# Column order of the output products, and the start of the large tiles, in an attention and expert kernel

## The chip, the core and the metric

The kernel runs on one core of one Trainium2 chip. The metric is the device time of one execution in microseconds (us); lower is better.

## The reference

Four batches of 3008 tokens with 256 features go through squared-ReLU attention and then through one gated expert layer:

```python
scores = (1 / S) * z @ z.T            # per batch, z is S x 64, S = 3008
attn = maximum(scores, 0) ** 2
x = u * (attn @ v)                    # S x 256
xn = x / rms(x) * g
g_ = xn @ w_gate                      # 256 x 1536
val = xn @ w_val                      # 256 x 1536
out = (silu(g_) * val) @ w_out        # 1536 x 256
```

All inputs and the output are float32.

## The kernel before, in words

The tokens of a batch are taken in pairs of chunks, 1024 tokens at a time (960 in the last pair of a batch): 12 pairs. A pair has two phases. Phase A is attention: for each of 24 blocks of 128 keys the scores are formed (L456, L457), squared, split into a rounded high part and the rest, and multiplied with the values (L585, L586, L590), which are split in the same way. Phase M is the expert layer, 12 units per pair: a unit takes 128 of the 1536 hidden features. With a seven-product scheme for 2 x 2 blocks it forms gate and value of both halves of the pair (L792 to L794; three matmuls to a product, for the high and low parts of weights and of tokens), applies SiLU, multiplies, and splits the result into a high part hH (ScalarE, L804) and a low part hL (VectorE, L809). All these matmuls take float32r operands and are written out in full precision into PSUM.

The change touches the output products, `Unit.y(h)`, called for h = 0 and h = 1. It multiplies the 128 hidden features of the unit with w_out and adds into two accumulators (d = 0, 1, 128 output features each) that stay open over the 12 units of a pair. Each call issues six matmuls: L820 (high weights woh, hH) and L821 (low weights wol, hH) for d = 0, the same for d = 1, then L824 (woh, hL) for both d. n is the number of moving columns, 512, or 480 in the last pair of a batch. The calls wait in a queue, `pend`, and are popped between the products of the next unit (L880, L886), so the order of matmuls on TensorE (PE) is written out by hand. After the last unit the accumulators are copied out (L833, L835) and stored (L836).

PE runs its instructions in the order written. Loads of weights and data come by DMA from SyncE's queue. The remaining engines form the scores' squares, splits and gates beside PE.

Memory: the tile pools lie one behind another in the order in which they are opened: const, keep, work, moving. Const holds front (96 floats), woh and wol (12,288 bytes each), misc and fold_sb (512 bytes each), in this order, per partition. Almost every tile of the other pools is 2048 or 4096 bytes long; the first tile of keep begins at byte 42,496, that is 41 x 1024 + 512, so these tiles all begin 512 bytes past a multiple of 1024. woh begins at 16,896, 512 past such a multiple too. fold_sb is read by one small matmul for each pair (L670). moving holds the tiles hH and hL (tags H and L) that the output products stream.

Of the kernel before, what the change touches and what calls it, by code (L numbers as in the profile page):

```python
# [8 lines left out]
F32 = mybir.dt.float32  # L9
# [10 lines left out]
P = 128  # L20
# [10 lines left out]
def kernel(  # L31
# [13 lines left out]
    nc = tc.nc  # L45
# [5 lines left out]
    NF = DFF // P  # L51
# [17 lines left out]
    const = ctx.enter_context(tc.tile_pool(name="const", bufs=1))  # L69
    keep = ctx.enter_context(tc.tile_pool(name="keep", bufs=1))  # L70
    work = ctx.enter_context(tc.tile_pool(name="work", bufs=1))

    moving = ctx.enter_context(tc.tile_pool(name="moving", bufs=1))
    ps_s = ctx.enter_context(tc.tile_pool(name="ps_s", bufs=4, space=bass.MemoryType.PSUM))
    ps_a = ctx.enter_context(tc.tile_pool(name="ps_a", bufs=1, space=bass.MemoryType.PSUM))
    dram = ctx.enter_context(tc.tile_pool(name="dram", bufs=1, space=bass.MemoryType.DRAM))
# [4 lines left out]
    def where(p):  # L81

        b, j = divmod(p, NP)
        return b, 2 * j, b * S + j * PAIR, min(PAIR, S - j * PAIR)
# [5 lines left out]
    woh = const.tile([P, NF, D], F32R, name="woh")  # L90
    wol = const.tile([P, NF, D], F32R, name="wol")
    misc = const.tile([P, P], F32, name="misc")
    g_sb, warm = front[:, :ND], front[:, ND:ND + 1]
    fold_sb = const.tile([P, P], F32, name="fold_sb")

    jobs = defaultdict(list)

# [110 lines left out]
    def prep_proj(j, pool, tags):  # L208
# [35 lines left out]
        def combine(key, x, y, op, into=None):  # L244
            def go():
                out = w[into] if into is not None else work.tile([P, CH], F32, tag="ws", name="ws")
                pool_pieces(out, w[x], w[y], op)
                w[key] = out
            return go
# [319 lines left out]
    acc = {}  # L569
# [64 lines left out]
    def norm_jobs(p):  # L634
# [3 lines left out]
        q = {}  # L638
        small = misc.rearrange("p (k a) -> p k a", a=PAIR // BLK)
        m, y, w, pp = (small[:, k, :nb] for k in range(4))  # L640
        x = [ux[p, d] for d in range(ND)]

# [36 lines left out]
        def cubic():  # L679
            nc.vector.tensor_tensor(w, m, y, op=ALU.mult)  # L680
            yield
            nc.vector.tensor_tensor(w, w, y, op=ALU.mult)
            yield
            nc.vector.tensor_scalar(pp, w, 0.375, -1.25, op0=ALU.mult, op1=ALU.add)
            yield
            nc.vector.tensor_tensor(pp, pp, w, op=ALU.mult)
            yield
            nc.vector.scalar_tensor_tensor(y, pp, 1.875, y, op0=ALU.add, op1=ALU.mult)
# [94 lines left out]
    class Unit:  # L783
# [28 lines left out]
        def y(self, h):  # L812
            p, f, n = self.p, self.f, self.n
            if f == 0:
                for d in range(ND):
                    acc[h, d] = ps_a.tile([P, CH], F32, tag=f"acc{h}{d}", name="py")
            hi, lo = self.h[h]
            for d in range(ND):
                ds = slice(d * P, (d + 1) * P)
                nc.tensor.matmul(acc[h, d][:, :n], woh[:, f, ds], hi[:, :n], start=(f == 0), stop=False)  # L820
                nc.tensor.matmul(acc[h, d][:, :n], wol[:, f, ds], hi[:, :n], start=False, stop=False)  # L821
            for d in range(ND):
                ds = slice(d * P, (d + 1) * P)
                nc.tensor.matmul(acc[h, d][:, :n], woh[:, f, ds], lo[:, :n], start=False, stop=(f == NF - 1))  # L824
            if f == NF - 1:
                t0 = where(p)[2] + h * n
                for d in range(ND):
                    if p == NPAIR - 1 and h == d == 1:
                        out = work.tile([P, CH], F32, tag="T", name="y", bufs=6)
                    else:  # L830
                        out = work.tile([P, CH], F32, tag="out", name="y", bufs=3)
                    if d == 0:
                        nc.scalar.copy(out[:, :n], acc[h, d][:, :n])  # L833
                    else:
                        nc.vector.tensor_copy(out[:, :n], acc[h, d][:, :n])  # L835
                    nc.sync.dma_start(out=outT[d * P:(d + 1) * P, t0:t0 + n], in_=out[:, :n])  # L836
# [172 lines left out]
    for p in range(NPAIR):  # L1009
        b, c0 = where(p)[:2]  # L1010
# [79 lines left out]
    for p in range(1, NPAIR):  # L1090
# [12 lines left out]
        start = 1  # L1103
# [5 lines left out]
        elif p == 2:  # L1109
            start = 4  # L1110
        elif p == NPAIR - 1:
            at(m.phase, 0, lambda p=p: load_x(p))
            start = 3
        h = m.put(jobs_, start)
# [133 lines left out]
```

## Time and profile before

| | |
|---|---|
| two timed executions | 2022.31 and 2023.12 us, median 2022.71 |
| span of the profiled execution (first to last instruction) | 2020.6 us |
| its own time apart from the span | not listed |
| mean granted TensorE clock | 0.999 |
| PE busy | 2006.9 us, 99% |
| VectorE (DVE) busy | 1604.6 us, 79% |
| ScalarE (ACT) busy | 1413.7 us, 70% |
| GpSimd (POOL) busy | 227.5 us, 11% |

PE's matmuls are pipelined: a matmul's duration in the profile reaches past the start of the next one. A rate is therefore read from the starts of successive matmuls. PEld is PE's loading of weights, which runs beside the matmuls. In the rows, "128x512 f32" behind a matmul is its output, 128 partitions by 512 columns. L820 is line 820 of the kernel before.

### The profile page before, as it was taken

How to read it: one execution, taken by the hardware profiler on the slowest of the kernel's cores; microseconds unless marked ns; L12 is line 12 of the kernel's file. 1: busy time of each engine (PE TensorE's matmuls, PEld its weight loads, DVE VectorE, ACT ScalarE, POOL GpSimd, SP SyncE). 2: the span in 40 equal slices, each digit the busy share in tenths (PEclk: the TensorE clock that was granted, in tenths of full speed). 3: DMA queues.
4: the chain of work that ended last, by engine and by line, in shares of the span. 5: the costliest groups of instructions: out<-in, count | busy, mean ns of one | idle time of the engine just before them, and what ended most of it. 6: DMA issues, size and time to landing. Idle time of an engine off the chain costs nothing.

```text
span 2020.6 us, 27263 instructions
## 1 busy us (share of the span) xinstructions
PE 2006.9 (99%) x8976; PEld 1675.6 (83%) x8976; DVE 1604.6 (79%) x2693; ACT 1413.7 (70%) x2580; POOL 227.5 (11%) x376
## 2 busy tenths in 40 slices
PE   9999999999999999999999999999999999999999
PEld 7787878888888888888888888888888888888887
DVE  8989978987867768787786877888778777777765
ACT  8888867886765656796586665779658656566665
POOL 0547905000000001300000000320000000000000
PEclk9999999999999999999999999999999999999999
DMA  5135575373494697246348478625536747734342
GB/s 173 48 112 169 133 241 172 136 233 128 113 237 151 158 204 238 102 170 215 125 132 233 139 160 228 213 102 189 180 120 184 205 135 181 196 128 165 115 147 93
DMA packets 352367, 328.38 MB, mean 163 GB/s; under 512 B 221536, under 2 KB 268256, under 8 KB 352224
## 3 DMA queue, kind: packets, MB, share of 16 engines
q1 hardware_dynamic: 352224, 326.64, 53.6%
q8 instruction: 70, 1.15, 0.2%
q14 instruction: 73, 0.60, 0.1%
HBM read 189.73 MB, written 85.72 MB: 136 GB/s over the span
## 4 chain that ended last, share of the span: by engine, by line
PE 92%; DMA 2%; DVE 2%; issue 1%; POOL 1%; ACT 1%; SPq 0%; DVEq 0%; POOLq 0%; ACTq 0%
PE po L585 11%; PE po L586 11%; PE ps L793 11%; PE ps L792 11%; PE po L590 11%; PE ps L794 11%; PE py L820 6%; PE py L821 6%; PE py L824 6%; PE ps L457 4%; PE ps L456 4%; DMA wu<-wc 1%; POOL w L140 1%; POOL wolo L140 1%; DVE L L508 0%
## 5 line engine op out<-in xcount | busy, mean ns | idle before, releaser
L585 PE MATMUL po<-H,vh 128*128 128x512 f32 (+1 forms) x1152 | 446.7, 388 | 1.9 <-DVE y L835 1.0
L586 PE MATMUL po<-H,vl 128*128 128x512 f32 (+1 forms) x1152 | 445.0, 386 | 0.0
L799 ACT COPY s<-ps 128x512 f32<-128x512 f32 (+1 forms) x432 | 249.6, 578 | 215.2 <-PE ps L794 214.6
L793 PE MATMUL ps<-xh,wu 128*128 128x512 f32 (+1 forms) x1008 | 389.3, 386 | 1.7 <-DMA wu<-wc 1.6
L792 PE MATMUL ps<-xh,wu 128*128 128x512 f32 (+1 forms) x1008 | 390.0, 387 | 0.5 <-DMA wu<-wc 0.5
L794 PE MATMUL ps<-xl,wu 128*128 128x512 f32 (+1 forms) x1008 | 388.6, 386 | 0.0
L590 PE MATMUL po<-L,vh 128*128 128x512 f32 (+1 forms) x1104 | 336.5, 386 | 3.1 <-DVE L L508 2.9
L804 ACT CAST hH<-s 128x512 fp32r<-128x512 f32 (+1 forms) x288 | 176.6, 613 | 194.5 <-DVE s L891 187.5
L809 DVE TENSOR_TENSOR hL<-s,hH 128x512 fp32r<-128x512 f32 (+1 forms) x288 | 200.0, 694 | 100.0 <-ACT hH L804 88.6
L468 ACT ACTIVATE r<-ps 128x512 f32<-128x512 f32 x354 | 195.9, 595 | 105.3 <-PE ps L457 87.6
L585 PEld LDWEIGHTS po<-H,vh 128*128 128x128 f32 x1152 | 216.3, 188 | 45.9 <-ACT H L495 2.1
L586 PEld LDWEIGHTS po<-H,vl 128*128 128x128 f32 x1152 | 216.5, 188 | 39.8
L475 DVE TENSOR_TENSOR r<-ps,r 128x512 f32<-128x512 f32 (+1 forms) x287 | 186.5, 681 | 73.1 <-ACT r L468 72.3
L590 PEld LDWEIGHTS po<-L,vh 128*128 128x128 f32 x1104 | 206.5, 188 | 45.4 <-DVE L L508 6.5
L508 DVE TENSOR_TENSOR L<-r,H 128x512 fp32r<-128x512 f32 (+1 forms) x334 | 226.7, 712 | 9.7 <-ACT r L502 7.5
L820 PE MATMUL py<-hH,woh 128*128 128x512 f32 (+1 forms) x576 | 222.2, 386 | 0.1
L821 PE MATMUL py<-hH,wol 128*128 128x512 f32 (+1 forms) x576 | 222.0, 385 | 0.0
L793 PEld LDWEIGHTS ps<-xh,wu 128*128 128x128 f32 x1008 | 189.2, 188 | 38.8 <-DMA wu<-wc 3.7
L792 PEld LDWEIGHTS ps<-xh,wu 128*128 128x128 f32 x1008 | 189.2, 188 | 38.8 <-ACT s L799 1.9
L794 PEld LDWEIGHTS ps<-xl,wu 128*128 128x128 f32 x1008 | 189.2, 188 | 35.9
L370 POOL TENSOR_TENSOR vl<-raw,vh 128x128 fp32r<-128x128 f32 x144 | 78.8, 586 | 938.5 <-ACT vh L359 484.4
L824 PE MATMUL py<-hL,woh 128*128 128x512 f32 (+1 forms) x576 | 175.3, 385 | 0.0
(96 smaller groups left out, 2973.7 us busy)
## 6 DMA issues: line engine op xcount, KB each, us to landing
wu<-wc SPq DMA_DIRECT2D x288, 448.0 KB, 4.0
kept<-halves SPq DMA_DIRECT2D x168, 256.0 KB, 2.2
raw<-in_v SPq DMA_DIRECT2D x44, 256.0 KB, 3.5
raw<-in_zT SPq DMA_DIRECT2D x38, 256.0 KB, 4.5
u<-in_uT SPq DMA_DIRECT2D x36, 256.0 KB, 4.6
xg<-u SPq DMA_DIRECT2D x36, 256.0 KB, 2.2
out_T<-y SPq DMA_DIRECT2D x32, 256.0 KB, 2.0
ux<-xg SPq DMA_DIRECT2D x14, 512.0 KB, 4.4
```

Of the source, the lines that this page charges most:

```text
L508: nc.vector.tensor_tensor(lo[:, :n], a[:, :n], f32(hi[:, :n]), op=ALU.subtract)
L585: nc.tensor.matmul(po[d][:, :n], wh[:, j, ds], hi[:, :n], start=(i == 0), stop=False)
L586: nc.tensor.matmul(po[d][:, :n], wl[:, j, ds], hi[:, :n], start=False, stop=(ends and lo is None))
L590: nc.tensor.matmul(po[d][:, :n], wh[:, j, ds], lo[:, :n], start=False, stop=ends)
L792: nc.tensor.matmul(ps[:, :n], wh[:, o, :], xh[:, :n], start=start, stop=False, skip_group_check=True)
L793: nc.tensor.matmul(ps[:, :n], wl[:, o, :], xh[:, :n], start=False, stop=False, skip_group_check=True)
L794: nc.tensor.matmul(ps[:, :n], wh[:, o, :], xl[:, :n], start=False, stop=stop, skip_group_check=True)
L799: nc.scalar.copy(s, ps[:, :self.n])
L809: nc.vector.tensor_tensor(lo[:, :self.n], s, f32(self.h[h][0][:, :self.n]), op=ALU.subtract)
L820: nc.tensor.matmul(acc[h, d][:, :n], woh[:, f, ds], hi[:, :n], start=(f == 0), stop=False)
L821: nc.tensor.matmul(acc[h, d][:, :n], wol[:, f, ds], hi[:, :n], start=False, stop=False)
L824: nc.tensor.matmul(acc[h, d][:, :n], woh[:, f, ds], lo[:, :n], start=False, stop=(f == NF - 1))
```

## The change

The three kinds of output product pass over the n columns in other orders than from left to right. The moving operand and the accumulator are permuted alike, so each column's sum still lands in its place. L820 takes the four quarters in the order 0, 2, 1, 3. L821 takes four columns of the first half, then four of the second half, and so on. L824 does the same with n / 16 columns at a time (32, or 30 where n is 480). And fold_sb moves from the pool const to a pool of its own, top, that is opened behind moving, so that keep, work and moving begin 512 bytes earlier.

```diff
     moving = ctx.enter_context(tc.tile_pool(name="moving", bufs=1))
+    top = ctx.enter_context(tc.tile_pool(name="top", bufs=1))
...
-    fold_sb = const.tile([P, P], F32, name="fold_sb")
+    fold_sb = top.tile([P, P], F32, name="fold_sb")
...
             hi, lo = self.h[h]
+            def lines(t):
+                return t[:, :n].rearrange("p (a b c) -> p b a c", a=2, b=2)
+
+            def turns(t, c):
+                return t[:, :n].rearrange("p (h a c) -> p a h c", h=2, c=c)
+
+            wide = n // 16
             for d in range(ND):
                 ds = slice(d * P, (d + 1) * P)
-                nc.tensor.matmul(acc[h, d][:, :n], woh[:, f, ds], hi[:, :n], start=(f == 0), stop=False)
-                nc.tensor.matmul(acc[h, d][:, :n], wol[:, f, ds], hi[:, :n], start=False, stop=False)
+                nc.tensor.matmul(lines(acc[h, d]), woh[:, f, ds], lines(hi), start=(f == 0), stop=False)
+                nc.tensor.matmul(turns(acc[h, d], 4), wol[:, f, ds], turns(hi, 4), start=False, stop=False)
             for d in range(ND):
                 ds = slice(d * P, (d + 1) * P)
-                nc.tensor.matmul(acc[h, d][:, :n], woh[:, f, ds], lo[:, :n], start=False, stop=(f == NF - 1))
+                nc.tensor.matmul(
+                    turns(acc[h, d], wide), woh[:, f, ds], turns(lo, wide), start=False, stop=(f == NF - 1)
+                )
```

## Rows read from the trace of the kernel before

**Rows 1.** The page: busy time of each engine, granted clock in 40 slices
```profile
PE 2006.9 (99%) x8976; PEld 1675.6 (83%) x8976; DVE 1604.6 (79%) x2693; ACT 1413.7 (70%) x2580; POOL 227.5 (11%) x376
...
PEclk9999999999999999999999999999999999999999
```
**Rows 2.** The page: the chain that ended last, by engine and line
```profile
PE 92%; DMA 2%; DVE 2%; issue 1%; POOL 1%; ACT 1%; SPq 0%; DVEq 0%; POOLq 0%; ACTq 0%
PE po L585 11%; PE po L586 11%; PE ps L793 11%; PE ps L792 11%; PE po L590 11%; PE ps L794 11%; PE py L820 6%; PE py L821 6%; PE py L824 6%; PE ps L457 4%; PE ps L456 4%; DMA wu<-wc 1%; POOL w L140 1%; POOL wolo L140 1%; DVE L L508 0%
```
**Rows 3.** PE's waits, longest and shortest of nine: total us, times, longest
```profile
PE po L590 <- DVE L L508: 2.9, 4, 1.1
...
PE po L585 <- DVE u L622: 0.2, 1, 0.2
```
**Rows 4.** Groups by shape, edited lines: count, busy us, mean ns, idle before
```profile
L820 PE MATMUL py<-hH,woh 128*128 128x512 f32 x384 | 149.5, 389 | 0.0
L821 PE MATMUL py<-hH,wol 128*128 128x512 f32 x384 | 149.4, 389 | 0.0
L824 PE MATMUL py<-hL,woh 128*128 128x512 f32 x384 | 118.3, 389 | 0.0
...
L821 PE MATMUL py<-hH,wol 128*128 128x480 f32 x192 | 72.6, 378 | 0.0
```
**Rows 5.** Busy time in a stretch of 512 and one of 480 columns
```profile
core 0: us, PE busy (x) PEld busy (x) DVE busy (x) ACT busy (x) POOL busy (x), PEclk, DMA share, GB/s
999.66:1011.90 12.24, 12.24 (x55) 10.13 (x54) 8.08 (x13) 7.40 (x14) 0.00 (x0) 1.00 0.59 172
1989.65:2008.93 19.28, 19.28 (x90) 16.63 (x89) 11.91 (x19) 10.71 (x21) 0.00 (x0) 1.00 0.15 49
```
**Rows 6.** Timeline of PE, one group of output products: start us, us
```profile
1002.84 0.39 PE L820 MATMUL py<-hH,woh 128*128 128x512 f32 x1
...
1003.74 0.61 PE L824 MATMUL py<-hL,woh 128*128 128x512 f32 x2
1004.20 0.39 PE L792 MATMUL ps<-xh,wu 128*128 128x512 f32 x1
```
**Rows 7.** Timeline of PE, products of 256 and of 448 columns
```profile
126.40 0.28 PE L456 MATMUL ps<-woh,zst 128*128 128x256 f32 x1
...
126.64 0.40 PE L585 MATMUL po<-H,vh 128*128 128x512 f32 x1
...
265.74 0.36 PE L585 MATMUL po<-H,vh 128*128 128x448 f32 x1
...
266.95 0.40 PE L792 MATMUL ps<-xh,wu 128*128 128x512 f32 x1
```
**Rows 8.** Groups by shape: ScalarE, contiguous and stepped reads
```profile
L799 ACT COPY s<-ps 128x512 f32<-128x512 f32 x288 | 169.1, 587 | 142.0 <-PE ps L794 141.6
L561 ACT COPY halves<-r 128x1024 uint16<-128x1024 uint16 x102 | 107.1, 1060 | 1.9 <-DMA out_T<-y 1.8
L652 ACT ACTIVATE q<-ux 128x512 f32<-128x512 f32 x40 | 23.7, 629 | 8.4 <-DMA ux<-xg 5.6 <-DVE misc L664 1.5 <-DVE q L660 1.4
L157 ACT ACTIVATE w<-wraw 128x512 f32<-128x512 f32 x12 | 8.1, 678 | 2.5 <-DMA wraw<-in_w_val 2.5
```
**Rows 9.** Timeline of PE, the first nine matmuls
```profile
1.48 3.40 PE L124 MATMUL ps<-idle 128*128 128x512 f32 x8 [1.48 <-DVE idle L121]
4.86 0.50 PE L456 MATMUL ps<-mh,zst 128*128 128x512 f32 x1
```
**Rows 10.** Weight loads of L793 and L586: ns min/median/max, first, last start
```profile
L793 PEld LDWEIGHTS ps<-xh,wu x1008: 186/188/192, 263.1 to 2011.5; 128*128 128x128 f32 x168
...
L586 PEld LDWEIGHTS po<-H,vl x1152: 186/188/192, 9.8 to 1756.8; 128*128 128x128 f32 x192
```
**Rows 11.** Groups by shape: VectorE, L758, 480 columns
```profile
L758 DVE TENSOR_TENSOR xl<-ux,xh 128x480 fp32r<-128x480 f32 x16 | 10.4, 651 | 0.3 <-ACT xh L753 0.3
L758 DVE TENSOR_TENSOR xl<-xc,xh 128x480 fp32r<-128x480 f32 x12 | 7.8, 651 | 0.0
```

## The prediction

> **What bounds the kernel now.** I read the page first. [...] The reader is to see that 13.7 us of the span, 0.7%, is all that PE stands idle. The chain that ended last says the same from the other side: 92% of it is PE, and the three lines that the change edits, L820, L821 and L824, hold 6% each [rows 2]. PE's own list of waits adds up to 9.4 us, in nine entries of which the first and the last stand in [rows 3], 2.9 and 0.2 us. So whatever a matmul takes more or less stands one for one in the span; VectorE (79%) and ScalarE (70%) [rows 1] have room to follow.
>
> Next I asked what one matmul takes. The durations in the groups (389 ns) [rows 4] cannot be used: matmuls overlap, and the span holds 8976 of them, 225 ns each. The distance from start to start can. In a stretch with 512 columns only, 54 matmuls begin in 12.24 us (the row counts 55, one of them still running from before), 226.7 ns each; in a stretch with 480 columns, 89 in 19.28 us, 216.6 ns [rows 5]. Inside the first stretch one group of the edited lines, two L820, two L821 and two L824, goes from 1002.84 to 1004.20, 1.36 us or 226.7 ns each [rows 6]: the y products cost what every other product costs.
>
> [...]
>
> **The change part by part.** It adds and removes no instruction, no DMA, no wait, and moves nothing past a queue. It changes (a) the order in which 1728 matmuls read their moving tile and write their accumulator, and (b) the start of the tiles.
>
> (a) The edited lines have 384 matmuls each with 512 columns and 192 each with 480 [rows 4]: 1152 times 226.7 ns is 261.2 us, 576 times 216.6 is 124.8, together 386.0 us of the span. Each operand of one product is permuted alike, so the sums stay in place. L820 takes the quarters 0, 2, 1, 3: runs of 128 (120) columns and 3 breaks. L821 takes four columns from the first half, four from the second: 128 (120) runs, 127 (119) breaks. L824 takes sixteen runs of 32 (30): 15 breaks. Every run starts at an even column and has an even length; those of four fp32 are 16 bytes.
>
> The trace has no matmul that reads or writes in such an order (in the code before, each operand of a matmul is one run of columns), so the cost is bounded from both sides.
> [...]
> Loss, small end: ScalarE squares 512 contiguous elements in 629 ns and 512 taken every second element in 678 [rows 8], 8% more. Eight per cent of L821's third (128.7 us) is 10 us, of all three 31 us. ScalarE's copy that picks 16-bit halves out of a tile takes 1060 ns for 1024 elements, 1.04 ns each, against 587 for 512 contiguous ones, 1.15 each [rows 8]: no price at all.
> Loss, large end: the slowest full-size matmuls of the trace are the eight that open it, with PE idle for 1.48 us before: from their first start to the next product's start at 4.86 are 3.38 us, 422 ns each [rows 9]. If a run of four made a matmul that slow, L821 alone would cost (422 - 226.7) times 384 plus (396 - 216.6) times 192, with 396 for 480 columns in proportion: 75.0 + 34.4 = 109 us; all three lines three times that, 328 us.
> I take zero. Of these rows the copy of halves is nearest in kind (a reordered read without arithmetic), and the runs here keep at least four neighbours together where ScalarE's dear case keeps one.
>
> [...]
>
> (b) fold_sb is 128 floats, 512 bytes in each partition. With it out of the pool of constants, everything allocated behind that pool (keep, work, moving) begins 512 bytes earlier; front, woh, wol and misc lie ahead of it and stay. For the weights the trace already has both kinds of start: wu is cut in steps of 512 bytes, vl too, and their loads take 186/188/192 ns at the least, median and most in 1008 and in 1152 cases [rows 10]. For VectorE, one subtraction reads ux at byte 1920 in part of its cases and xc at a tile's start: 651 ns both [rows 11]. So zero there. [...] I take zero, as the weight loads, also reads by PE, show no step.
>
> **Sum.** 0 + 0. The profiled execution's own time is not listed apart from its span, 2020.6 us; the two timed runs, 2022.31 and 2023.12, lie 1.7 and 2.5 us above that span, median 2.1. With that surround unchanged the forecast is 2020.6 + 2.1 = 2022.7 us, the median before. Where nothing else stalls, its own range is 2017 to 2028.
>
> **The rivals.**
> [...]
> *Short runs waste their reads* (the other side). Place: L821, perhaps the write into the accumulator. Price: up to 195 ns per matmul, 109 us, 2132; 2351 if all three lines suffer. It passes 2% (40.5 us) from 40.5 / 576 = 70 ns per L821 matmul. Nothing hides it, since PE has 0.7% idle [rows 1]. [...] Against it: a run of 16 bytes is four columns in a row, and the 127 breaks would have to cost half a nanosecond each for the point of decision, 1.5 for the whole. [...]
> [...]
> [...]
>
> **How the numbers follow.** Forecast 0.54; a cycle per break or a like small price 0.17; wasted reads above 2% 0.17; the y remainder gone 0.08; the new start felt everywhere 0.04. The range takes the first two and the fourth, 0.79, with their ends: 1997 to 2060. Two per cent is about what a measurement of this kernel can tell from no change. Faster by more than 2%: 0.04. Within: 0.54 + 0.17 + 0.08 = 0.79. Slower by more: 0.17. The value is that of the forecast.
>
> **What would show it.** If right, the six matmuls of a y group still take 1.36 us in the stretches of 512 columns, 226.7 ns from start to start on each of the three lines, and the groups L820, L821, L824 keep their means of 389 and about 378 ns. If breaks have a price, L821 shows it first and L820 hardly at all; a price per break makes L824's surplus about an eighth of L821's. [...] If the start matters, the lines that nobody edited (L792 to L794, L585 to L590) change their 226.7 ns. The forecast is wrong if any of these distances moves by more than 2 ns over the whole kernel, or if PE gains idle time, which no part of the change explains.

## The result and the profile after

The changed kernel takes 2041.35 us (2040.97 to 2041.72) against 2022.71: ratio 1.0094, 95% interval 1.0065 to 1.0123. It is 18.6 us slower, clear of noise and below 2%. The span of the profiled execution went from 2020.6 to 2039.2 us.

The page of the changed kernel, busy time, clock and the chain by line; the lines ahead of the edit have moved by 1, and L820, L821 and L824 are now L828, L829 and L832:
```profile
PE 2027.1 (99%) x8976; PEld 1677.1 (82%) x8976; DVE 1603.4 (79%) x2693; ACT 1416.0 (69%) x2580; POOL 226.8 (11%) x376
...
PEclk9999999999999999999999999999999999999999
...
PE ps L793 11%; PE ps L794 11%; PE ps L795 11%; PE po L586 11%; PE po L587 11%; PE po L591 10%; PE py L829 7%; PE py L832 6%; PE py L828 6%; PE ps L458 3%; PE ps L457 3%; DMA wu<-wc 1%; POOL wolo L141 1%; POOL w L141 1%; POOL ws L141 0%
```
Against [rows 1], PE is busy 20.2 us longer, no other engine by more than 2.3, and the clock stands where it was. PE's idle time did not grow (12.1 us, 13.7 before). So the matmuls themselves became longer, and in the chain it is the line of the fours, L829, that gained a per cent [rows 2].

The groups of the changed kernel by shape, edited lines (count, busy us, mean ns, idle before), which answer to [rows 4]:
```profile
L829 PE MATMUL py<-hH,wol 128*128 128x512 f32 x384 | 160.3, 417 | 0.0
L828 PE MATMUL py<-hH,woh 128*128 128x512 f32 x384 | 150.4, 392 | 0.0
L832 PE MATMUL py<-hL,woh 128*128 128x512 f32 x384 | 121.3, 397 | 0.0
L829 PE MATMUL py<-hH,wol 128*128 128x480 f32 x192 | 74.4, 388 | 0.0
L828 PE MATMUL py<-hH,woh 128*128 128x480 f32 x192 | 73.5, 383 | 0.0
L832 PE MATMUL py<-hL,woh 128*128 128x480 f32 x192 | 60.4, 396 | 0.0
```
A duration is not a rate, but its change comes near to one: the fours went from 389 to 417 ns, and by their starts, averaged over the trace, from 226.7 to 253.6. The readings below therefore go by the difference to the plain 389 ns (512 columns) or 378 to 379 (480) [rows 4], and name the starts where the two differ: for the dearest orders below, the durations overstate the price by up to 14 ns. At 512 columns the quarters cost 3 ns, the fours 28, the sixteenths 8. At 480 the order of cost turns round: fours 10 (7 by the starts), sixteenths 18 (16), quarters 4 (3).

The timeline of PE in the changed kernel, one group at 512 columns, as in [rows 6]:
```profile
1009.66 0.39 PE L828 MATMUL py<-hH,woh 128*128 128x512 f32 x1
1009.88 0.41 PE L829 MATMUL py<-hH,wol 128*128 128x512 f32 x1
1010.13 0.39 PE L828 MATMUL py<-hH,woh 128*128 128x512 f32 x1
...
1011.09 0.39 PE L793 MATMUL ps<-xh,wu 128*128 128x512 f32 x1
```
The six products take 1.43 us instead of 1.36. Added up from start to start over the whole trace, the output products take 386.3 us before and 405.6 after, 19.3 more; the experts' gate and value products (681.2 and 680.7), the products with the values (771.2 and 770.9) and the scores (171.0 both) moved by 0.5 us at most. The output products are the whole of the 18.6 us.

### The profile page after: what moved, and what is told of

Its sections match the earlier page's. It is cut to its first block, busy times and chain, and to the rows that moved or that the text cites. A ratio compares the mean times of both kernels' runs of the same rounds, so it can differ in the third digit from the quotient of the medians.

```text
span 2039.2 us, 27263 instructions
## 1 busy us (share of the span) xinstructions
PE 2027.1 (99%) x8976; PEld 1677.1 (82%) x8976; DVE 1603.4 (79%) x2693; ACT 1416.0 (69%) x2580; POOL 226.8 (11%) x376
## 4 chain that ended last, share of the span: by engine, by line
PE 92%; POOL 2%; DMA 2%; issue 2%; DVE 1%; ACT 1%; SPq 0%; POOLq 0%; DVEq 0%; ACTq 0%
PE ps L793 11%; PE ps L794 11%; PE ps L795 11%; PE po L586 11%; PE po L587 11%; PE po L591 10%; PE py L829 7%; PE py L832 6%; PE py L828 6%; PE ps L458 3%; PE ps L457 3%; DMA wu<-wc 1%; POOL wolo L141 1%; POOL w L141 1%; POOL ws L141 0%
## 5 line engine op out<-in xcount | busy, mean ns | idle before, releaser
L586 PE MATMUL po<-H,vh 128*128 128x512 f32 (+1 forms) x1152 | 446.5, 388 | 1.9 <-DVE ux L623 0.8
L793 PE MATMUL ps<-xh,wu 128*128 128x512 f32 (+1 forms) x1008 | 390.9, 388 | 0.0
L586 PEld LDWEIGHTS po<-H,vh 128*128 128x128 f32 x1152 | 216.3, 188 | 45.8 <-ACT H L496 2.5
L829 PE MATMUL py<-hH,wol 128*128 128x512 f32 (+1 forms) x576 | 234.7, 408 | 0.0
L828 PE MATMUL py<-hH,woh 128*128 128x512 f32 (+1 forms) x576 | 223.9, 389 | 0.0
L793 PEld LDWEIGHTS ps<-xh,wu 128*128 128x128 f32 x1008 | 189.2, 188 | 39.0 <-ACT s L800 1.5
L832 PE MATMUL py<-hL,woh 128*128 128x512 f32 (+1 forms) x576 | 181.8, 396 | 0.0
```

The lines of the kernel that those rows point to most:

```text
L586: nc.tensor.matmul(po[d][:, :n], wh[:, j, ds], hi[:, :n], start=(i == 0), stop=False)
L793: nc.tensor.matmul(ps[:, :n], wh[:, o, :], xh[:, :n], start=start, stop=False, skip_group_check=True)
L828: nc.tensor.matmul(lines(acc[h, d]), woh[:, f, ds], lines(hi), start=(f == 0), stop=False)
L829: nc.tensor.matmul(turns(acc[h, d], 4), wol[:, f, ds], turns(hi, 4), start=False, stop=False)
L832: nc.tensor.matmul(turns(acc[h, d], wide), woh[:, f, ds], turns(lo, wide), start=False, stop=(f == NF - 1))
```

## The experiments

**Orders and start apart.** Two theories: the orders cost by themselves, or only because the tiles now begin on multiples of 1024 bytes.

The first run takes back the pool:
```diff
-    fold_sb = top.tile([P, P], F32, name="fold_sb")
+    fold_sb = const.tile([P, P], F32, name="fold_sb")
```


> The three new orders with fold_sb back in const, so that every tile begins where it did before (512 past a multiple of 1024). Theory A, the orders alone cost: the whole 18.6 us stays, 2041 us (2038 to 2044), and the products of four columns keep about 254 ns from start to start at 512 columns. Rival B, the halves collide only because the tiles now begin on multiples of 1024: 2023 to 2030 us, those products back below 235 ns.

Measured 2041.75 us, ratio 1.0089 (1.0074 to 1.0104). The run with the orders alone, groups by shape:
```profile
L829 PE MATMUL py<-hH,wol 128*128 128x512 f32 x384 | 160.3, 417 | 0.0
L828 PE MATMUL py<-hH,woh 128*128 128x512 f32 x384 | 150.4, 392 | 0.0
L832 PE MATMUL py<-hL,woh 128*128 128x512 f32 x384 | 121.3, 397 | 0.0
```
These are the rows of the changed kernel to the nanosecond. The second run keeps the pool and takes back the orders:
```diff
-                nc.tensor.matmul(lines(acc[h, d]), woh[:, f, ds], lines(hi), start=(f == 0), stop=False)
+                nc.tensor.matmul(acc[h, d][:, :n], woh[:, f, ds], hi[:, :n], start=(f == 0), stop=False)
...
```


> fold_sb in the pool top, so that all moving tiles begin on multiples of 1024, and the three products in plain order. Theory A, the orders alone cost: 2022.7 us as before (2020 to 2025), every product 226.7 ns at 512 columns. Rival B, the start has a share of its own: over 2026 us, seen as a longer distance on lines that nobody edited.

Measured 2023.13 us, ratio 1.000 (0.999 to 1.001). The move of the tiles' start by 512 bytes costs and gives nothing; the orders are the whole change.

**Read or write.** An order stands on both operands. Each run below leaves it on one; the other side runs from left to right.
```diff
-                nc.tensor.matmul(turns(acc[h, d], 4), wol[:, f, ds], turns(hi, 4), start=False, stop=False)
+                nc.tensor.matmul(acc[h, d][:, :n], wol[:, f, ds], turns(hi, 4), start=False, stop=False)
...
```


> Only the reads of the moving tiles keep the new orders; the accumulators are written from left to right, so the kernel's output has its columns mixed. Theory R, the price is on the read from SBUF: 2041 us, with four columns about 254 ns at 512 columns and sixteenths about 235. Theory W, it is on the write to PSUM: 2023 us, all near 227 ns. Theory P, a price of the access pattern itself, paid once on whichever side has one: 2041 here and in the run with the writes alone.

> The mirror of the run before: the moving tiles are read from left to right, the accumulators written in the new orders, so the output's columns are mixed. Theory R (read side): 2023 us, all products near 227 ns at 512 columns. Theory W (write side): 2041 us, four columns near 254 ns. Theory P (the pattern itself): 2041 us as well.

Reads alone: 2042.74 us, ratio 1.0094 (1.0074 to 1.0114). Writes alone: 2022.95 us, 0.9994 (0.9984 to 1.0004). The run with the reads alone, groups by shape:
```profile
L829 PE MATMUL py<-hH,wol 128*128 128x512 f32 x384 | 160.3, 417 | 0.0
...
L832 PE MATMUL py<-hL,woh 128*128 128x512 f32 x384 | 121.3, 397 | 0.0
```
The run with the writes alone:
```profile
L829 PE MATMUL py<-hH,wol 128*128 128x512 f32 x384 | 149.4, 389 | 0.0
...
L832 PE MATMUL py<-hL,woh 128*128 128x512 f32 x384 | 118.2, 389 | 0.0
```
All of it is on the read of the moving tile; theories W and P fall. A third run looked for the write's limit, with runs of two columns:
```diff
+            def turned(t, q):
+                k, c = q
+                return t[:, :n].rearrange("p (h a c) -> p a h c", h=k, c=c)
...
+                if f % 6 == 0:
+                    q = (2, 2) if n == CH else (2, 2)
+                    nc.tensor.matmul(turned(acc[h, d], q), w, plain(x, q), start=first, stop=end)
...
```


> Writes alone: accumulators written in runs of two columns, with jumps of 1024, 512, 256, 64 and 16 bytes, and of four columns with 1024, going round with the unit (the output's columns are mixed). Theory N, an order of writes in pairs costs nothing: 2023 us, 227 ns at 512 columns in all six. Rival, a broken order on the PSUM side costs below four columns: runs of two over 250 ns, over 2040 us.

Measured 2023.73 us, against 2022.87 beside it, one execution of each. (The runs below with a single time are one execution too; there the rows of the groups carry the reading, not the total.) The writes of pairs, groups by shape, pairs 1024 bytes and 16 bytes apart:
```profile
L832 PE MATMUL py<-hH,woh 128*128 128x512 f32 x64 | 24.9, 390 | 0.0
L844 PE MATMUL py<-hH,woh 128*128 128x512 f32 x64 | 24.9, 389 | 0.0
```
That is the plain time, 389 ns [rows 4], so theory N holds: down to pairs, a broken order of the writes costs nothing here. No run writes single columns in turns.

**Run length.** The same helper, on the reads alone, going round with the unit.

> Reads alone, always two halves in turns, the run length going round with the unit: 1, 2, 4, 8, 16, 32 columns where n is 512; 30, 24, 20, 12, 10, 6 where n is 480 (the output's columns are mixed). Theory T1, a fixed price per break of 0.21 ns (27 ns over 127 breaks): at 512 columns +107, +54, +27, +13, +7, +3 ns over 227. Theory T2, a price per 16-byte line that is not read whole: runs of 1 and 2 cost by far the most (over +150 and over +75 ns), 4 to 32 are all whole lines and cost the same +27 or less; at 480 columns the runs that are no multiple of 4 columns (30, 10, 6) cost more than their neighbours 24, 20, 12, though 24 and 20 have more breaks than 30.

Measured 2068.77 us. Reads in runs, groups by shape. At 512 columns L832, L835, L838, L841, L844, L847 are runs of 1, 2, 4, 8, 16, 32; at 480 columns, in the same order, of 30, 24, 20, 12, 10, 6:
```profile
L835 PE MATMUL py<-hH,woh 128*128 128x512 f32 x64 | 32.3, 505 | 0.0
L838 PE MATMUL py<-hH,woh 128*128 128x512 f32 x64 | 26.8, 419 | 0.0
L841 PE MATMUL py<-hH,woh 128*128 128x512 f32 x64 | 25.9, 405 | 0.0
...
L847 PE MATMUL py<-hH,woh 128*128 128x512 f32 x64 | 25.5, 398 | 0.0
L832 PE MATMUL py<-hH,woh 128*128 128x512 f32 x64 | 24.2, 378 | 0.0
L847 PE MATMUL py<-hH,woh 128*128 128x480 f32 x32 | 14.7, 458 | 0.0
L844 PE MATMUL py<-hH,woh 128*128 128x480 f32 x32 | 13.4, 417 | 0.0
L832 PE MATMUL py<-hH,woh 128*128 128x480 f32 x32 | 12.6, 395 | 0.0
...
L841 PE MATMUL py<-hH,woh 128*128 128x480 f32 x32 | 12.2, 382 | 0.0
L835 PE MATMUL py<-hH,woh 128*128 128x480 f32 x32 | 12.1, 379 | 0.0
```
At 480 columns the prices lie as theory T2 had them: runs of 6, 10 and 30, no multiples of four columns (16 bytes), cost 80, 39 and 17 ns; runs of 12, 20 and 24, which are, cost 1 to 4, though 12 has more breaks than 30. At 512 columns, from runs of 2 to runs of 32, the price is 116 (110 by the starts), 30, 16, 14 and 9. It does not halve with each step, as T1 would have it, nor do the runs of four and more all cost the same, as T2 would have it. And single columns in turns (L832), which both theories made the dearest, take 378 ns, 11 *less* than the plain order.

**Distance.** Runs of four, the halves replaced by more and nearer places:

> Reads alone, always runs of four columns, the distance of the jump going round with the unit: 1024, 512, 256, 128, 64, 32 bytes where n is 512; 640, 480, 240, 384, 320, 192 bytes where n is 480 (the output's columns are mixed). Theory T1, a price per break wherever it jumps to: +27 ns at 512 columns at every distance. Theory T3, lines that lie a certain distance apart collide: +27 or more at 1024, 512 and 256 bytes, falling to +5 or less at some shorter distance; at 480 columns, where 960 bytes cost only 7 ns, distances that are odd multiples of 64 bytes (192, 320, 960) stay below +10 and 384 and 640, even multiples, cost more.

Measured 2052.08 us. Fours by distance, groups by shape. L832, L835, L838, L841, L844, L847 are 1024, 512, 256, 128, 64, 32 bytes at 512 columns; the last row shown is L838 at 480 columns, 240 bytes:
```profile
L838 PE MATMUL py<-hH,woh 128*128 128x512 f32 x64 | 28.2, 441 | 0.0
L835 PE MATMUL py<-hH,woh 128*128 128x512 f32 x64 | 27.7, 433 | 0.0
L832 PE MATMUL py<-hH,woh 128*128 128x512 f32 x64 | 26.5, 414 | 0.0
L841 PE MATMUL py<-hH,woh 128*128 128x512 f32 x64 | 26.1, 408 | 0.0
L847 PE MATMUL py<-hH,woh 128*128 128x512 f32 x64 | 25.2, 394 | 0.0
L844 PE MATMUL py<-hH,woh 128*128 128x512 f32 x64 | 24.8, 387 | 0.0
L838 PE MATMUL py<-hH,woh 128*128 128x480 f32 x32 | 12.2, 382 | 0.0
```
T1 falls: the same number of breaks costs 52, 44, 25, 19, 5 or nothing. At 480 columns all six distances, 384 and 640 bytes among them, lie at 379 to 382 ns, so the guess about multiples of 64 bytes falls too. What fits is narrower: in the four dear patterns an address comes soon after another that lies 1024 bytes from it; at 480 columns no two nearby ones do. That is an argument from the patterns, and it does not say why steps of 256 bytes, where three other places lie between the two, cost twice what 1024 bytes cost. It is tried once more below.

To see whether it was the distance or the number of columns, one run reads 480 columns in both kinds of pair, leaving 32 columns of the product out in the larger one:
```diff
+            def fours(t, x):
+                halves = t[:, :2 * x].rearrange("p (h x) -> p h x", h=2)[:, :, :m // 2]
+                return halves.rearrange("p h (a c) -> p a h c", c=4)
...
+                elif f % 6 == 1:
+                    nc.tensor.matmul(a[:, :m], w, fours(x, 256), start=first, stop=end)
...
```


> In the pairs of 1024 tokens the units after the first multiply only 480 of the 512 columns (the rest of the product is left out): going round with the unit, from left to right, or in fours from two places in turns that lie 1024, 1008, 992, 976 or 960 bytes apart. Reads alone are turned; the pairs of 960 tokens stay plain. Theory T3, lines 1024 bytes apart collide: fours at 1024 bytes cost 20 to 28 ns over the plain 480 columns, the other four distances under 8. Rival, what saved the pairs of 960 tokens was their number of columns: all five distances cost alike, under 10 ns. Second rival, the price follows the distance in small steps: falling from 1024 to 960.

Measured 2027.90 us; the time itself tells little, since columns are left out. Fours at one width, groups by shape; L830 is the plain order in the smaller pairs, L834, L836, L838, L840 and L842 are 1024, 1008, 992, 976 and 960 bytes:
```profile
L830 PE MATMUL py<-hH,woh 128*128 128x480 f32 x192 | 72.8, 379 | 0.1
L834 PE MATMUL py<-hH,woh 128*128 128x480 f32 x64 | 25.7, 402 | 0.0
L836 PE MATMUL py<-hH,woh 128*128 128x480 f32 x64 | 25.1, 392 | 0.0
...
L840 PE MATMUL py<-hH,woh 128*128 128x480 f32 x64 | 24.9, 390 | 0.0
L842 PE MATMUL py<-hH,woh 128*128 128x480 f32 x64 | 24.9, 389 | 0.0
```
At equal width 1024 bytes cost 23 ns, the other four 10 to 13 (21, and 9 to 12, by the starts). So 1024 is special, as T3 has it, and neither rival holds: the five do not cost alike, and the price falls in one step and then hardly. But about half of it is there at any of these distances, more than the 8 that T3 allowed.

**One kind at a time.** Each third of the units turns one of the three products only.
```diff
+                if k in (0, 2) and f % 3 == 0:
+                    nc.tensor.matmul(lines(a), w, lines(x), start=first, stop=end)
+                elif k in (1, 3) and f % 3 == 1:
...
```


> The output is the reference's. A third of the units has the quarters order on its first kind of product alone, a third the order of fours on the second kind alone, a third the order of sixteenths on the third kind alone; all else in plain order. If the three prices add up: one third of 18.6 us, 2029 us (2027 to 2031). If the quarters cost nothing of their own and their 3 ns is the tail of the product of fours ahead of them: 227 ns for the quarters, about 254 for the fours and 231 for the plain product right behind one; sixteenths 235 at 512 and 233 at 480 columns. Rival, the price needs a change of order between neighbours: the quarters show 5 ns or more as well.

Measured 2034.33 us, not 2029. One kind at a time, groups by shape (L831 quarters, L833 fours, L835 sixteenths, L837 plain):
```profile
L837 PE MATMUL py<-hL,woh 128*128 128x512 f32 x256 | 79.9, 393 | 0.0
L833 PE MATMUL py<-hH,wol 128*128 128x512 f32 x128 | 53.4, 418 | 0.0
L831 PE MATMUL py<-hH,woh 128*128 128x512 f32 x128 | 50.2, 392 | 0.0
```
Fours (418) and quarters (392) are as they were, but plain products of hL among them now take 393: a turned product also delays plain ones that follow. So the three prices do not add up to thirds. The timeline of the same run tells the kinds apart; first a group of six with the quarters alone, then one with the fours alone:
```profile
999.74 0.39 PE L831 MATMUL py<-hH,woh 128*128 128x512 f32 x1
...
1001.10 0.39 PE L793 MATMUL ps<-xh,wu 128*128 128x512 f32 x1
...
1001.78 0.39 PE L837 MATMUL py<-hH,woh 128*128 128x512 f32 x1
...
1002.75 0.63 PE L837 MATMUL py<-hL,woh 128*128 128x512 f32 x2
1003.22 0.39 PE L793 MATMUL ps<-xh,wu 128*128 128x512 f32 x1
```
The six products with the quarters take 1.36 us, as before the change. With the fours alone they take 1.44, though four of the six are plain: averaged over all such groups of 512 columns 1436.1 ns, no less than a group of the changed kernel with all three orders (1436.1; 1360.8 before). The plain hL products behind the fours take 237 and 233 ns, about what the sixteenths take in that place (236 and 233). So at 512 columns the fours alone bring the whole price, and the sixteenths, which alone cost a group 17.7 ns, add nothing behind them. The quarters have no price of their own at 512 columns: where the nearest turned products lie some 20 matmuls back they take 227 ns, and only a few matmuls behind sixteenths 236 and 232; that is the second of the theories. At 480 columns a group loses 14 ns by the quarters alone, 18 by the fours, 31 by the sixteenths, and 51 by all three in the changed kernel. Three plain products behind a group of sixteenths also take 4 to 7 ns more, so of the 12.0 us by which the span grew, the output products hold 8.5 and the gate, value and score products 3.5. How a turned product slows the plain ones behind it, no run here shows.

**Single columns.** The gain seen above, put to the test with other steps, and in a version that computes the reference.

> Reads alone, single columns in turns, so that successive columns lie a step apart: 1024, 512, 128, 32, 16 and 8 bytes where n is 512, 960, 480, 120, 32, 16 and 8 where n is 480, going round with the unit (the output's columns are mixed). In the run-length run single columns 1024 bytes apart took 216 ns, 11 less than the plain order. Theory U, any step other than one column spares what the plain order loses: 216 ns at all six steps, and about 203 at 480 columns. Theory V, only two places in turns do it, since both lines are still at hand: 216 at 1024, dearer than 227 from 512 down to 16 where each column is on another line, and at 8 bytes about 227.

Measured 2280.27 us. Single columns, groups by shape; L832, L835, L838, L847 are steps of 1024, 512, 128 and 8 bytes at 512 columns, the last row is 960 bytes at 480:
```profile
L847 PE MATMUL py<-hH,woh 128*128 128x512 f32 x64 | 40.3, 629 | 0.0
L838 PE MATMUL py<-hH,woh 128*128 128x512 f32 x64 | 38.8, 606 | 0.0
L835 PE MATMUL py<-hH,woh 128*128 128x512 f32 x64 | 28.0, 437 | 0.0
L832 PE MATMUL py<-hH,woh 128*128 128x512 f32 x64 | 24.2, 379 | 0.0
...
L832 PE MATMUL py<-hH,woh 128*128 128x480 f32 x32 | 11.7, 366 | 0.0
```
Theory U falls. Theory V holds in its times but for its 8-byte guess (240 ns dearer): two places in turns gain 10 ns at 512 and 12 at 480 columns (11 and 14 by the starts), four places cost 48, and from sixteen on the price is 213 or more (202 by the starts). V's reason, that both lines are still at hand, is not shown; runs of two from two places, which cost 116, speak against it. The version with the gain in the three output products and the columns put back in order when the accumulators are copied out:
```diff
+            def single(t):
+                return t[:, :n].rearrange("p (h a) -> p a h", h=2)
...
+                nc.tensor.matmul(acc[h, d][:, :n], woh[:, f, ds], single(hi), start=(f == 0), stop=False)
...
+                        nc.scalar.copy(whole_(out), back(acc[h, d]))
```


> The output is the reference's: all three kinds of output product read single columns of the two halves in turns, write from left to right, and the columns are put back in order by the two copies out of the accumulators. From the run-length run: 1152 products at 512 columns, each 11 ns shorter, 12.7 us; if 480 columns gain as much in proportion, 6 us more: 2004 us, 2010 if they gain nothing. Rival, the 216 ns were an effect of the units around it: 2023 us or more. Second rival, the copies out, 48 of them, cost more with a step: at most 0.6 us each where PE waits for them, under 10 us.

Measured 2005.40 us, ratio 0.9917 (0.9901 to 0.9934). By their starts the output products sum to 365.4 us, 20.9 less than before, 11 ns on 1152 and 14 on 576; the net gain is 16.8. Of the 4 us between, the trace shows 2.5 in the other products, whose starts add up to 1.1 us more in gate, value and scores and 1.4 more in the products with the values; the span of the profiled execution, the fastest of the four, falls by 18.3; the rest lies between executions. The first rival falls. So does the second: the 48 copies out take 30.4 us together instead of 30.1. Then the same for the moving operands of all these products, scores and values included:
```diff
+    def single(t, n, k=0):
+        return t[:, :n].rearrange("p (h a) -> p a h", h=2)[:, k // 2:, :]
...
-            nc.tensor.matmul(po[d][:, :n], wh[:, j, ds], hi[:, :n], start=(i == 0), stop=False)
+            nc.tensor.matmul(po[d][:, :n], wh[:, j, ds], single(hi, n), start=(i == 0), stop=False)
...
-            nc.vector.tensor_tensor(x[:, :n], acc[k, d][:, :n], x[:, :n], op=ALU.mult)
+            nc.vector.tensor_tensor(blocks_of(x, n), mixed(acc[k, d], n), blocks_of(x, n), op=ALU.mult)
...
```


> The output is the reference's, by the kernel before with every moving operand read in single columns of its two halves in turns: the queries are stored with even and odd columns apart, the other products let their columns come out mixed, and the gate and the copies out put them in order. From the runs so far: 11 ns less on 6668 products of 512 columns, 14.6 on 1584 of 480, about 13 on 616 of 448, together 73 + 23 + 8 = 104 us: 1918 us (1910 to 1930). Rival, ScalarE and VectorE, 70 and 79% busy before, come late more often when PE is 5% quicker: 1930 to 1960 us, with PE idle over 20 us. Second rival, the attention's products do not gain: about 1960 us.

Measured 1949.34 us, ratio 0.964 (0.9624 to 0.9656): the best of all. The page of this version, busy time, then PE's waits (total us, times, longest), the two longest:
```profile
PE 1915.8 (98%) x8976; PEld 1679.4 (86%) x8976; DVE 1605.4 (82%) x2693; ACT 1407.3 (72%) x2580; POOL 237.9 (12%) x376
```
```profile
PE po L599 <- DVE L L517: 9.0, 12, 1.7
PE ps L802 <- DMA wu<-wc: 5.0, 8, 1.0
```
PE's busy time fell by 91.1 us, of the 104 forecast, and 18.5 us of that came back as idle time (32.2 us now, 13.7 before): VectorE is late for L599 9.0 us in all instead of 2.9 [rows 3], and the loads of wu for L802 5.0. So the gain falls 31 us short. The rates do not: taken from start to start, an undelayed product takes 215.8 ns at 512 columns, 202.4 at 480 and 189 at 448, near enough as forecast, the attention's products too, so the second rival falls. The products start too late: what the starts lose against these rates adds up to 55 us, against 24 before by the rates of that kernel, and the 31 us of difference are the whole gap. The largest parts are 11.5 us at L599 (VectorE), 7.4 at L802 (the DMA of wu) and 6.5 at L594. The idle time shows 18.5 of them only, because a matmul's duration reaches some 160 ns past the next start and hides a late start of that size. The first rival is thus right in its range and its idle time, with the weights' DMA beside the engines that it named.

## Why the prediction was wrong, by its steps

**What bounds the kernel: right.** PE is the bound, and what 1728 matmuls lost, 19.3 us from start to start, stands nearly whole in the span, 18.6. That a matmul's gain stands there one for one as well held for a small gain (18.3 of 20.9 us in the first version with single columns) and not for a large one (73 of 104 in the second).

**(a), "I take zero": wrong; this step failed.** Between the two ends the choice went to ScalarE's copy of halves as the nearest row [rows 8]. That row told nothing of PE's read: the runs show a price of 19.3 us in its place, all of it on the read of the moving tile. By the lines' starts the fours cost 27 ns at 512 columns (384 x 27 = 10.3 us) and 7 at 480 (1.3), the sixteenths 8 (3.0) and 16 (3.0), the quarters 3 (1.6 in all). By cause the share is another: 192 groups of 512 columns lose 75.3 ns each, 14.46 us, and the fours alone bring that; the 96 groups of 480 lose 50.6 ns each, 4.86 us, to all three kinds.

**"A cycle per break or a like small price", 0.17: right in sign, wrong in kind.** The upper end of the range, 2060, rests on an estimate of mine of what one break costs; no run shows it. The mark of a price per break, that the sixteenths' surplus is an eighth of the fours', failed: turned alone, they cost a group 17.7 ns against 75 at 512 columns, and 31 against 18 at 480. And the same number of breaks cost between nothing and 52 ns, by their distance. The runs put in its place a price of the read by where its runs lie, 18.6 us of the time: more when places 1024 bytes apart follow each other directly (23 against 10 to 13 ns at one width), and more when a run is no multiple of 16 bytes (17 to 80 against 1 to 4 ns at 480 columns).

**"Short runs waste their reads": not at four columns, but it exists.** The point of decision, 70 ns, was not reached at four; by the starts, runs of two cost 110 and single columns from sixteen places 204. That this lies near the large end of 195 taken from [rows 9] is chance: those eight matmuls read their columns from left to right, so no order made them slow.

**"The y remainder gone", 0.08: not by the orders of this change, but there was something to gain.** The lower end of the range, 1997, rests on an estimate of mine of the least that a product can take; no row of the kernel before shows it. What the runs show in its place: products read in single columns take 215.8 ns at 512 columns and 202.3 at 480, 11 and 14 less than in the plain order, and these belong to the order of the read. For the output products alone the net gain was 16.8 us.

**(b), zero: right**, by the run with the start alone, ratio 1.000. So a new start felt everywhere, at a chance of 0.04, is out as well.

**"Perhaps the write into the accumulator": wrong side of the matmul.** The writes alone cost nothing in any order tried (2022.95 us, ratio 0.9994; in pairs 389 to 390 ns at 512 columns).

## What to carry to other kernels

Where PE is the bound, read its rate from the starts of successive matmuls and try the read in another order, even where the rate looks like a fixed price: here it stood near 227 ns on every line at 512 columns, and fell to 215.8 by the order of the read. A row of one engine is no nearest row for another engine's access to the same memory. And an order of columns can be chosen freely as long as some other instruction, off the bound, makes or undoes it: in the last version VectorE's busy time went from 1604.6 to 1605.4 us for it and ScalarE's from 1413.7 to 1407.3.

## What the runs showed of the hardware that I had not expected

Two single columns in turns, 1024 or 960 bytes apart, are read faster than neighbours: 215.8 against 226.7 ns at 512 columns of float32r and 202.3 against 216.6 at 480, while four places take 277 and sixteen 431 at 512, all by the starts. At 480 columns, runs of 6, 10 and 30 columns, no multiples of four (16 bytes), cost 75, 36 and 16 ns by the starts, and runs of 12, 20 and 24 no more than 4 by their durations. Counted from their order, the three dear ones go to a block of four columns 40, 24 and 8 times more often than runs of whole blocks would. That count does not explain both runs of two (two visits to a block, 110 ns dearer) and single columns in turns (four visits, 11 ns faster). Why the plain order loses 11 ns, and why runs of two cost so much more than single columns, no run here settles.
